# Ten feed-forward steps of a Mamba-2 plus gated FFN kernel: seven 128-wide products for eight in the first matrix product

## The chip, the core and the metric

The kernel runs on one core of one Trainium2 chip. The metric is the device time of one execution in microseconds (us); the runs of the kernel before took 368.01, 369.35 and 369.48 us, the median is 369.35.

Engines are named as in the profile: PE (TensorE matmuls), PEld (its weight loads), DVE (VectorE, called V in the code), ACT (ScalarE), POOL (GpSimd, called G), SP (the queue of most DMAs).

## The reference, cut to what matters

```python
# x: (4, 8, 768, 32), a: (4, 8, 768), B and C: (4, 8, 768, 16)
# w_in: (256, 2048), w_out: (2048, 256), all float32
def reference(x, a, B, C, w_in, w_out):
    y = mamba2_ssd(x, a, B, C)              # a scan in chunks; per chunk y_intra + y_inter
    t = y.transpose(0, 2, 1, 3).reshape(4 * 768, 256)
    h = t @ w_in                            # 3072 x 2048
    g = h * cos(h)
    return g @ w_out                        # 3072 x 256
```

The change concerns `h = t @ w_in` for part of the tokens.

## The kernel before

The 768 positions are cut into six chunks (NC = 6) of 128, for all four batches together: 512 tokens a chunk. The feed-forward part of a chunk takes 16 steps (NF = 16), so there are 96 steps, n = 0 to 95. From chunk 1 on, a step (u, j) takes one half u of the chunk's tokens (4 batches x 64 positions = 256 tokens) and 256 of the 2048 inner columns (pair j of eight). In it:

- `first(n)` (L659) computes hp(n), 256 inner columns x 256 tokens over 256 model columns, as a 128 x 512 tile of one PSUM bank: four matmuls of 128 x 256. The profile counts each float32 matmul as two records, so eight. The banks of hp have the tag "h", of which there are two, so hp(n) needs the bank that hp(n-2) leaves.
- `wind(n)`: ACT makes the whole number of turns k from hp (L666), DVE the remainder w (L672).
- `gate(n)`: ACT takes the sine, which is cos(h) (L681).
- `gated(n)`: DVE multiplies, gT = hp * cos (L686). This is the last reader of hp(n). Then POOL makes four sums and differences of the four 128 x 128 quarters of gT(n) in three instructions (`differ`: L711, L713, L714).
- `seven(n)` (L767) multiplies gT by w_out. It does a product of 2 x 2 blocks in seven block products instead of eight (the Winograd form of Strassen's scheme): 7 matmuls of 128 x 128, 14 records. It runs two steps late (LAG = 2), so PE's order is hp(n), seven(n-2), hp(n+1), seven(n-1), and so on. The seven partial results of eight steps stay in two PSUM banks; after the eighth (j = 7) ACT copies them to SBUF (L776, L777) and, in a later step, DVE adds them up in four instructions (L784) and SP sends them out (L787). These four additions are held in the list `unsummed`; steps with f = 10 and 11 leave it alone.

The order on every engine is the order in which the Python loop at the end of the kernel emits the calls, since the scheduling is by hand (`manual_schedule`). For step n of the last chunk the loop emits: first(n), wind(n), gate(n), gated(n), then `unsummed`, then seven(n-2). So DVE's queue is w(n), gT(n), [L784 x4], w(n+1), gT(n+1), and ACT's is k(n), sine(n), [L776, L777], k(n+1), sine(n+1). The scan of a chunk (lines L375 to L629: decays, reach, turned, state, g, y) is worked off in the steps of the chunk before, so the last chunk's 16 steps, n = 80 to 95, have only feed-forward work. Steps 88 to 95 ("final") keep their partial results in three banks: `shared` (L798 to L803) adds up what both output halves need before the last step, and `last_step` (L811, L814, L816) does step 95 with eight plain matmuls.

The w_in and w_out tiles lie in SBUF for the whole kernel. The four combinations of w_out that `seven` needs are made by POOL in steps 14 to 22 (`differ_w`, L705).

Of the kernel before, what the change touches and what calls it, by code (L numbers as in the profile page):

```python
# [8 lines left out]
FP32 = mybir.dt.float32  # L9
# [16 lines left out]
def kernel(  # L26
# [42 lines left out]
    def bank(shape, name, tag):  # L69
        return psum.tile(shape, FP32, tag=tag, bufs=2, name=name)  # L70

    def pair(name):

        return psum.tile([P, 2, 4 * P], FP32, tag="scan", bufs=2, name=name)
# [570 lines left out]
    def turn_of(n):  # L645

        c, f = divmod(n, NF)
        return (f % 2, f // 2) if c == 0 else divmod(f, NJ)
# [30 lines left out]
    def gate(n):  # L679
        cos = turns[n]  # L680
        ACT.activation(cos, cos, AF.Sin, bias=quarter, scale=TWO_PI)  # L681
# [25 lines left out]
    def differ(n):  # L707
# [5 lines left out]
        G.tensor_tensor(out=d[:, 2], in0=g[:, 0], in1=d[:, 0], op=ALU.subtract)  # L713
        G.tensor_tensor(out=d[:, 3], in0=g[:, 2], in1=d[:, 2], op=ALU.subtract)  # L714

    unit_rows = out.rearrange("(s q k i) m -> q k i s m", s=2, q=2, i=W)

    def second(n):
# [20 lines left out]
    def seven(n):  # L739

        c = n // NF
        u, j = turn_of(n)
        final = n >= NC * NF - NJ
        if j == 0:


            if final:
                lo, hi = (pair("o")[:, 0].rearrange("p (q m) -> p q m", m=P) for _ in range(2))
                mid = bank([P, 4, P], "o", "o")
                o[c, u] = (mid, lo, hi, {1: mid[:, 0], 6: mid[:, 1], 7: mid[:, 2], 5: mid[:, 3],  # L750
                                         2: lo[:, 0], 3: lo[:, 1], 4: hi[:, 0]})
            else:
                lo, hi = (bank([P, 4, P], "o", "o") for _ in range(2))
                o[c, u] = (lo, hi, {1: lo[:, 0], 6: lo[:, 1], 2: lo[:, 2], 7: hi[:, 0],
                                    5: hi[:, 1], 4: hi[:, 2], 3: hi[:, 3]})
        at = o[c, u][-1]
        g = gT.pop(n)
        if n == NC * NF - 1:
            last_step(g, *o[c, u][1:3])
            return  # L760
        d = gd.pop(n)
        w = {1: w4[:, j, 0, 0], 2: w4[:, j, 1, 0], 3: w4[:, j, 1, 1], 4: wd[3][:, j],
             5: wd[0][:, j], 6: wd[2][:, j], 7: wd[1][:, j]}
        a_ = {1: g[:, 0], 2: g[:, 2], 3: d[:, 3], 4: g[:, 3], 5: d[:, 0], 6: d[:, 2], 7: d[:, 1]}
        starts = (1, 2, 4) if final else (1, 7)
        for q in (1, 2, 6, 7, 5, 4, 3):
            PE.matmul(at[q], lhsT=a_[q], rhs=w[q], start=(j == 0 and q in starts),  # L767
                      stop=(j == NJ - 1), skip_group_check=True)
        if final and j == NJ - 2:
            shared(o[c, u][0])  # L770
        if j < NJ - 1:
            return

        sum_ = two.tile([P, 7, P], FP32, tag="sum", bufs=1, name="sum")
        ps = two.tile([P, 7, P], FP32, tag="ps", bufs=1, name="ps")
        ACT.copy(out=ps[:, 0:3], in_=o[c, u][0][:, 0:3])  # L776
        ACT.copy(out=ps[:, 3:7], in_=o[c, u][1])  # L777

        def rest():
            for dst, a_, b_ in ((sum_[:, 0:2], ps[:, 1:3], ps[:, 0:1]),  # L780
                                (sum_[:, 5:7], ps[:, 3:5], sum_[:, 0:1]),
                                (sum_[:, 3:5], ps[:, 5:3:-1], sum_[:, 5:6]),
                                (sum_[:, 2:3], ps[:, 6:7], sum_[:, 6:7])):
                V.tensor_tensor(out=dst, in0=a_, in1=b_.to_broadcast([P, dst.shape[1], P]),  # L784
                                op=ALU.add)
            for s in range(2):
                nc.sync.dma_start(out=unit_rows[s, 2 * c + u], in_=sum_[s * W:(s + 1) * W, 1:5].rearrange(  # L787
                                      "p (t h) m -> p t (h m)", t=2))

        unsummed.append(rest)  # L790
# [151 lines left out]

    AHEAD = 4

    def first_steps():

        grade("in", 1)
        for q in range(2):
            weights(1, q)
        states_of = []  # L950
        first(0, lambda: states_of.extend(finish0(1)))
        take_s1, add_s1 = states_of
        join("in", 1)
        rests = [grade("out", 0, later=True)]
        wind_k(0)
        take_s1()
        rests.pop()()
        wind_w(0)
        first(1)
        join("out", 0)  # L960
        wind_k(1)
        gate(0)
        wind_w(1)
        gate(1)
        gated(0)
        gated(1)
        first(2, tag=None)
        rests = [grade("in", 2, later=True)]
        wind_k(2)
        rests.pop()()  # L970
        clip_cut()
        wind_w(2)
        rests = [grade("out", 1, later=True)]
        join("in", 2)
        first(3, tag=None)
        gate(2)
        wind_k(3)
        rests.pop()()
        rests = [grade("in", 3, later=True)]
        gated(2)  # L980
        join("out", 1)
        second(0)
        wind_w(3)
        gate(3)
        rests.pop()()
        rests = [grade("out", 2, later=True)]
        join("in", 3)
        gated(3)
        second(1)
        clip_all()  # L990
        return add_s1, rests
# [7 lines left out]
    for n in range(AHEAD, NC * NF + LAG):  # L999
        c, f = divmod(n, NF)  # L1000
        if n < NC * NF:

            if c > 0 and f in (loads_of := (6, 7, 8, 9) if c == 1 else (0, 1, 2, 3)):
                load(c + 2, loads_of.index(f))
            if n in (NF - 4, NF - 3):
                load_arow(n - NF + 8)
            if n == NF - 2:
                for k in (4, 5):
                    for s in range(2):
                        load_x(k, s)  # L1010
            if n in (NF - 1, NF):
                load_along(2, (2 * (n == NF), 2 * (n == NF) + 1))
            for e, i in chunks_at(n, "along"):
                load_along(e + 1, (2 * i, 2 * i + 1))
            first(n)
            closing = f == NF - 1 and 1 <= c < NC - 1
            take_y = finish2(c + 1) if closing else None
            wind(n)
            if closing:
                take_y(0)  # L1020
            for e, s in chunks_at(n - 1, "turn"):
                turn2(e, s)
            for k in units_at(n, 2):
                turn_unit(k)
            if n + 1 in piece:
                rests_of.append(grade(*piece[n + 1], later=True))
            gate(n)
            while len(rests_of) > (n == AHEAD):
                rest = rests_of.pop(0)
                if rest:  # L1030
                    rest()
            joins = n in piece and piece[n] in held
            if joins:
                join(*piece[n])

            behind = [lambda at=at: decays2(*at) for at in decays_at(n)]
            behind += [lambda k=2 * c - 1 + i: add_state(k) for c, i in chunks_at(n, "state")]
            behind += [lambda c=c, b=2 * s + p: reaches(c, b) for c, s in chunks_at(n, "reach")
                       for p in range(2)]
            behind += [lambda at=at: turn_blocks(*at) for at in chunks_at(n, "turn")]  # L1040
            behind += [lambda k=k, p=p: decays0(k, p) for k, at in unit_at.items()
                       for p in range(2) if at[0][p] == n]
            behind = [lambda k=2 * c + i, q=q: weights(k, q) for c, i in chunks_at(n, "weigh")
                      for q in range(2)] + behind
            behind = [lambda k=k: weights(k, 1) for k in units_at(n - 1, 3)] + behind
            if not joins and behind:
                behind.pop(0)()
            gated(n)
            if closing:
                take_y(1)  # L1050
            if n == NF + 7:
                weigh0(5)
            if add_s and (n == NF - 5 or units_at(n - 1, 4)):
                exchange = add_s()
                add_s = None
            if n == NF + 9:
                exchange()
            for do in behind:
                do()
            if f not in ((10, 11, 12) if c == 1 else (10, 11)):  # L1060
                for do in unsummed:
                    do()
                unsummed.clear()
            for k, ((_, last_), *_) in unit_at.items():
                if last_ == n:
                    weigh0(k)
        for i, js in differ_at.get(n, ()):
            differ_w(i, js)
        if n == AHEAD + 1:
            second(AHEAD - LAG)  # L1070
        if n >= LAG and n != AHEAD:
# [53 lines left out]
```

## Time and profile before

| | before |
|---|---|
| device time, median of three runs | 369.35 us (368.01 to 369.48) |
| the profiled execution: device time | 367.37 us |
| its span, first to last instruction | 365.2 us |
| around the span | 2.17 us |
| PE busy | 359.7 us (98%) |
| DVE busy | 249.6 us (68%) |
| POOL busy | 204.5 us (56%) |
| ACT busy | 177.8 us (49%) |
| mean granted TensorE clock | 0.999 |

The page of the profile describes one execution. Busy time counts neither waiting nor DMA issue. In a group of instructions, `out<-in` names the tiles, then come the shape, the count, the busy time, the mean ns of one, and after the bar the idle time of the engine just before these instructions with what ended it. In a timeline each line gives the start (us from the start of the span), the duration, the engine, the line, the operation and the count.

### The profile page before, as it was taken

What the parts mean: (1) busy time and instruction counts of PE and PEld (TensorE: products, weight loads), DVE (VectorE), ACT (ScalarE), POOL (GpSimd) and SP (SyncE); (2) the same over time, 40 slices, a digit from 0 to 9 for tenths busy, and PEclk for the clock granted to TensorE, in tenths of its full rate; (3) what the DMA queues carried; (4) which work ended last, traced back from release to release, by engine and by line L of the source; (5) the groups of instructions that cost most, each with busy time, mean ns of one, the idle gap of its engine ahead of it and who ended that gap; (6) DMA issues with size and microseconds to landing.
All of it is one profiled execution on the core that took longest, in us unless ns stands there. A gap on an engine that the chain in (4) does not pass through costs nothing.

```text
span 365.2 us, 9749 instructions
## 1 busy us (share of the span) xinstructions
PE 359.7 (98%) x3902; PEld 324.8 (89%) x3902; DVE 249.6 (68%) x420; ACT 177.8 (49%) x324; POOL 204.5 (56%) x331
## 2 busy tenths in 40 slices
PE   8999999999999999999999999999999999999995
PEld 5788888888999999999989999989999999999995
DVE  7799998488868747967735977754876363644463
ACT  4588766454454355534345444335553534443442
POOL 6567666679766544447734456744355443554441
PEclk9999999999999999999999999999999999999999
DMA  8997865692664455316034210010000010010011
GB/s 146 294 334 154 203 139 72 105 129 64 133 98 65 92 106 72 69 39 121 9 56 62 47 50 22 2 44 5 22 11 0 2 31 2 2 29 3 0 29 31
DMA packets 97324, 26.39 MB, mean 72 GB/s; under 512 B 87328, under 2 KB 93184, under 8 KB 97280
## 3 DMA queue, kind: packets, MB, share of 16 engines
q1 hardware_dynamic: 96032, 25.38, 34.6%
q8 instruction: 31, 0.51, 0.6%
q10 hardware_dynamic: 1248, 0.39, 0.5%
q14 instruction: 13, 0.11, 0.1%
HBM read 22.36 MB, written 3.34 MB: 70 GB/s over the span
## 4 chain that ended last, share of the span: by engine, by line
PE 89%; DVE 4%; POOL 3%; ACT 2%; issue 2%; ACTq 0%; POOLq 0%; DVEq 0%
PE hp L659 42%; PE o L767 33%; PE o L729 5%; PE y L629 2%; PE g L603 1%; PE y L477 1%; DVE mag L261 1%; PE y L617 1%; DVE mag L263 1%; POOL gd L711 1%; PE g L456 1%; PE a_ps L364 1%; PE warm L84 1%; DVE w L672 1%; POOL gd L713 1%
## 5 line engine op out<-in xcount | busy, mean ns | idle before, releaser
L659 PE MATMUL hp<-yT,w_in 128*128 128x256 f32 x768 | 182.7, 381 | 0.3 <-DVE gT L686 0.3
L659 PEld LDWEIGHTS hp<-yT,w_in 128*128 128x128 f32 x768 | 139.5, 190 | 18.2 <-issue 1.0
L711 POOL TENSOR_TENSOR gd<-gT 128x256 f32<-128x256 f32 x79 | 59.8, 757 | 111.9 <-DVE gT L686 102.5
L672 DVE SCALAR_TENSOR_TENSOR w<-hp,k 128x512 f32<-128x512 f32 x96 | 66.1, 688 | 71.4 <-ACT k L666 71.3
L681 ACT ACTIVATE w<-w,quarter 128x512 f32<-128x512 f32 x96 | 69.4, 723 | 71.8 <-DVE w L672 71.5
L666 ACT ACTIVATE k<-hp 128x512 int32<-128x512 f32 x96 | 57.2, 596 | 94.3 <-PE hp L659 94.1
L686 DVE TENSOR_TENSOR gT<-hp,w 128x512 f32<-128x512 f32 x96 | 65.6, 683 | 35.1 <-ACT w L681 33.2
L767 PE MATMUL o<-words,gd 128*128 128x128 f32 x474 | 65.9, 275 | 0.1
L767 PEld LDWEIGHTS o<-words,gd 128*128 128x128 f32 x474 | 59.3, 192 | 0.3 <-POOL gd L713 0.3
L767 PEld LDWEIGHTS o<-w_out,gT 128*128 128x128 f32 x316 | 47.2, 191 | 4.1
L767 PE MATMUL o<-w_out,gT 128*128 128x128 f32 x316 | 48.4, 276 | 0.0
L714 POOL TENSOR_TENSOR gd<-gT,gd 128x128 f32<-128x128 f32 x79 | 44.0, 557 | 6.2
L713 POOL TENSOR_TENSOR gd<-gT,gd 128x128 f32<-128x128 f32 x79 | 38.1, 483 | 6.2
L767 PE MATMUL o<-words,gT 128*128 128x128 f32 x158 | 30.6, 275 | 0.0
L767 PE MATMUL o<-w_out,gd 128*128 128x128 f32 x158 | 30.6, 275 | 0.0
L729 PE MATMUL o<-w_out,gT 128*128 128x256 f32 x128 | 29.9, 379 | 0.0
L375 DVE TENSOR_TENSOR_SCAN lam<-arow,unit 128x512 f32<-128x512 f32 x20 | 28.0, 1400 | 0.0
L729 PEld LDWEIGHTS o<-w_out,gT 128*128 128x128 f32 x128 | 24.2, 190 | 3.3
L767 PEld LDWEIGHTS o<-words,gT 128*128 128x128 f32 x158 | 24.0, 192 | 0.0
L767 PEld LDWEIGHTS o<-w_out,gd 128*128 128x128 f32 x158 | 24.0, 192 | 0.0
L465 DVE TENSOR_TENSOR m<-g,lam 128x512 f32<-128x512 f32 x24 | 16.2, 681 | 0.7 <-PE g L456 0.5
L784 DVE TENSOR_TENSOR sum<-ps,sum 128x256 f32<-128x256 f32 (+1 forms) x27 | 15.1, 586 | 0.6
(109 smaller groups left out, 274.7 us busy)
## 6 DMA issues: line engine op xcount, KB each, us to landing
words<-in_moe_w_in_dram SPq DMA_DIRECT2D x8, 512.0 KB
words<-in_moe_w_out_dram SPq DMA_DIRECT2D x8, 512.0 KB
xr<-in_x_dram SPq DMA_DIRECT2D x24, 128.0 KB
arow<-a_cut SPq DMA_DIRECT2D x10, 256.0 KB
arow<-a_cut SPq DMA_DIRECT2D x10, 252.0 KB
out_dram<-sum SPq DMA_DIRECT2D x18, 128.0 KB
bc<-in_B_dram SPq DMA_DIRECT2D x24, 64.0 KB
blocks<-in_B_dram SPq DMA_DIRECT2D x16, 32.0 KB
```

Of the source, the lines that this page charges most:

```text
L375: V.tensor_tensor_scan(out=lams[k][:, p, hs].rearrange(flat), data0=rows_.rearrange(flat), data1=unit0[:, hs].rearrange(flat), initial=0.0 ...
L465: V.tensor_tensor(out=m, in0=gs[k, q][:, :, 0:2 * P].rearrange("p k (s i) -> p k s i", s=2), in1=l, op=ALU.mult)
L659: PE.matmul(to_[:, e], lhsT=w_in[:, k, fs], rhs=y[:, k], start=(k == 0), stop=(k == KT - 1), skip_group_check=True)
L666: ACT.activation(k, hp[n], AF.Copy, bias=0.25, scale=INV_2PI)
L672: V.scalar_tensor_tensor(out=w, in0=hp[n], scalar=INV_2PI, in1=k, op0=ALU.mult, op1=ALU.subtract)
L681: ACT.activation(cos, cos, AF.Sin, bias=quarter, scale=TWO_PI)
L686: V.tensor_tensor(out=gT[n], in0=hp.pop(n), in1=cos, op=ALU.mult)
L711: G.tensor_tensor(out=d[:, 0:2], in0=g[:, 1:2].to_broadcast([P, 2, P]), in1=g[:, 3::-3], op=ALU.subtract)
L713: G.tensor_tensor(out=d[:, 2], in0=g[:, 0], in1=d[:, 0], op=ALU.subtract)
L714: G.tensor_tensor(out=d[:, 3], in0=g[:, 2], in1=d[:, 2], op=ALU.subtract)
L729: PE.matmul(o[c, u][:, t], lhsT=g[:, 2 * e + t], rhs=w_out[:, 2 * j + e], start=(j == e == t == 0), stop=(j == NJ - 1 and e == 1), skip_gr ...
L767: PE.matmul(at[q], lhsT=a_[q], rhs=w[q], start=(j == 0 and q in starts), stop=(j == NJ - 1), skip_group_check=True)
```

## The change

For steps 83 to 92 (`sevens`), hp(n) is computed by `first7` in seven products of 128 x 128 (14 records) instead of four of 128 x 256 (8 records).

- Four combinations of w_in (`wid`) are made by POOL: 16 instructions of 128 x 256, one in each step of chunk 3 (n = 48 to 63), behind `differ(n)` in the queue.
- Four combinations of yT (`yd`) are made by DVE in steps 80 and 81: four instructions of 128 x 256, two a step, behind gT.
- PE's order in a step is product 6 (to its own bank), 1 (to quarter 0 of the hp bank), 7, 5, 4 (to a third bank), 3 and 2 (to quarters 1 and 0 of the hp bank). ACT copies product 1 to SBUF after the second product. Then DVE makes the four quarters of hp in four instructions (128 x 128, 128 x 256, 128 x 256, 128 x 128); the third and fourth write into the hp bank. The two extra banks are the same for all ten steps, apart from one move of the first of them at step 91.
- In these steps gate and gated are emitted one step later: behind first(n+1), ahead of wind(n+1). So DVE's queue is sums(n), gT(n-1), w(n), sums(n+1), gT(n), w(n+1), and ACT's is copy(n), sine(n-1), k(n), copy(n+1).
- `unsummed` isn't worked off in these steps. What step 89 leaves is added up in step 93; before it was in step 92.
- In the final steps the three banks are laid out otherwise, and the products of `seven` are issued in the order 1, 2, 4, 6, 7, 5, 3 instead of 1, 2, 6, 7, 5, 4, 3.

```diff
+    win4 = w_in.rearrange("p k (j e f) -> p k j e f", j=NJ, e=2)
+    wid, yd = [], {}
+    def differ_in(i, js):
+        if i == len(wid):
+            t = conv.tile([P, 2 * WC, 2], U32, tag="words", bufs=8, name="wid")
...
+        g = [win4[:, k, js, e] for k in range(2) for e in range(2)]
+        a_ = (g[1], g[1], g[0], g[2])[i]
+        b_ = (g[3], g[0], wid[0][:, js], wid[min(i, 2)][:, js])[i]
+        G.tensor_tensor(out=wid[i][:, js], in0=a_, in1=b_, op=ALU.subtract)
+    def differ_y(c, i):
+        if i == 0:
+            yd[c] = ms[2].rearrange("p (i u m) -> p i u m", i=4, u=2)
...
+        V.tensor_tensor(out=d[:, i], in0=a_, in1=b_,
+                        op=ALU.add if i in (1, 2) else ALU.subtract)
+    def first7(n, at6, at):
+        c, f = divmod(n, NF)
+        u, j = turn_of(n)
+        hp[n] = bank([P, TB], "hp", "h")
+        to_ = hp[n].rearrange("p (q m) -> p q m", q=4)
...
+        dst = {6: at6, 1: to_[:, 0], 7: at[:, 0], 5: at[:, 1], 4: at[:, 2], 3: to_[:, 1],
+               2: to_[:, 0]}
+        def product(q):
+            PE.matmul(dst[q], lhsT=w[q], rhs=y_[q], start=(q in (6, 1, 7)), stop=True,
+                      skip_group_check=True)
+        parts = ms[3].rearrange("p (t q m) -> p t q m", t=2, q=4)[:, n % 2]
+        add = dict(op=ALU.add)
+        for q in (6, 1):
+            product(q)
+        ACT.copy(out=parts[:, 0], in_=to_[:, 0])
+        for q in (7, 5, 4, 3, 2):
+            product(q)
+        V.tensor_tensor(out=parts[:, 1], in0=at6, in1=parts[:, 0], **add)
+        V.tensor_tensor(out=parts[:, 2:4], in0=at[:, 0:2],
+                        in1=parts[:, 1:2].to_broadcast([P, 2, P]), **add)
+        V.tensor_tensor(out=to_[:, 2:4], in0=at[:, 2:0:-1],
+                        in1=parts[:, 2:3].to_broadcast([P, 2, P]), **add)
+        V.tensor_tensor(out=to_[:, 1], in0=to_[:, 1], in1=parts[:, 3], **add)
@@ seven
-                lo, hi = (pair("o")[:, 0].rearrange("p (q m) -> p q m", m=P) for _ in range(2))
-                mid = bank([P, 4, P], "o", "o")
+                t = pair("o").rearrange("p b (q m) -> p b q m", m=P)
+                mid, hi = t[:, 0], t[:, 1]
+                lo = bank([P, 4, P], "o", "o")
...
-        for q in (1, 2, 6, 7, 5, 4, 3):
+        for q in (1, 2, 4, 6, 7, 5, 3) if final else (1, 2, 6, 7, 5, 4, 3):
@@ ahead of the loop
+    sevens = range(NC * NF - 13, NC * NF - 3)
+    late, at_ = [], {}
+    def first_of_seven(n):
+        if n == sevens[0]:
+            at_.update(six=pair("m6")[:, 0, 0:P], rest=pair("m")[:, 0, 0:3 * P].rearrange(
+                "p (q m) -> p q m", m=P))
+        if n == NC * NF - NJ + LAG + 1:
+            at_["six"] = bank([P, 4, P], "m6", "o")[:, 0]
+        first7(n, at_["six"], at_["rest"])
+    def finish_late():
+        while late:
+            n = late.pop()
+            gate(n)
+            gated(n)
@@ in the loop
-            first(n)
+            if n in sevens:
+                first_of_seven(n)
+            else:
+                first(n)
+            finish_late()
...
-            gate(n)
+            if n not in sevens:
+                gate(n)
...
-            gated(n)
+            if n in sevens:
+                late.append(n)
+            else:
+                gated(n)
...
-            if f not in ((10, 11, 12) if c == 1 else (10, 11)):
+            for i in range(2):
+                if n in (sevens[0] - 3, sevens[0] - 2):
+                    differ_y(c, 2 * (n - sevens[0] + 3) + i)
+            if n not in sevens and f not in ((10, 11, 12) if c == 1 else (10, 11)):
                 for do in unsummed:
                     do()
...
+        if n // NF == NC - 3:
+            i, q = divmod(f, 4)
+            differ_in(i, slice(2 * q, 2 * q + 2))
```

More of the change, by code (lines that the diff above doesn't have):

```diff
@@ L714, in differ @@
         G.tensor_tensor(out=d[:, 3], in0=g[:, 2], in1=d[:, 2], op=ALU.subtract)
+    win4 = w_in.rearrange("p k (j e f) -> p k j e f", j=NJ, e=2)
[3 more added lines that the diff above has]
+            t = conv.tile([P, 2 * WC, 2], U32, tag="words", bufs=8, name="wid")
+            wid.append(t.rearrange("p a w -> p (a w)").bitcast(FP32)
+                       .rearrange("p (j f) -> p j f", j=NJ))
+        g = [win4[:, k, js, e] for k in range(2) for e in range(2)]
+        a_ = (g[1], g[1], g[0], g[2])[i]
+        b_ = (g[3], g[0], wid[0][:, js], wid[min(i, 2)][:, js])[i]
+        G.tensor_tensor(out=wid[i][:, js], in0=a_, in1=b_, op=ALU.subtract)
@@ new lines, in differ_y @@
+    def differ_y(c, i):
+        if i == 0:
+            yd[c] = ms[2].rearrange("p (i u m) -> p i u m", i=4, u=2)
+        d = yd[c]
+        y11, y12, y21, y22 = (yT[c][:, :, k, h * P:(h + 1) * P] for k in range(2) for h in range(2))
+        a_ = (y12, y22, y22, y21)[i]
+        b_ = (y11, y12, d[:, 0], d[:, 2])[i]
+        V.tensor_tensor(out=d[:, i], in0=a_, in1=b_,
[5 more added lines that the diff above has]
+        to_ = hp[n].rearrange("p (q m) -> p q m", q=4)
+        w = {1: win4[:, 0, j, 0], 2: win4[:, 1, j, 0], 3: wid[3][:, j], 4: win4[:, 1, j, 1],
+             5: wid[0][:, j], 6: wid[2][:, j], 7: wid[1][:, j]}
+        d, y = yd[c][:, :, u], yT[c][:, u].rearrange("p k (h i) -> p k h i", h=2)
+        y_ = {1: y[:, 0, 0], 2: y[:, 1, 0], 3: y[:, 1, 1], 4: d[:, 3], 5: d[:, 0], 6: d[:, 2],
+              7: d[:, 1]}
+        dst = {6: at6, 1: to_[:, 0], 7: at[:, 0], 5: at[:, 1], 4: at[:, 2], 3: to_[:, 1],
[16 more added lines that the diff above has]
+        V.tensor_tensor(out=to_[:, 1], in0=to_[:, 1], in1=parts[:, 3], **add)
```

## The prediction

> **What bounds the kernel now.** I read the page first (busy time by engine), then what TensorE waited for, then the chain that ended last.
>
> ```profile
> PE 359.7 (98%) x3902; PEld 324.8 (89%) x3902; DVE 249.6 (68%) x420; ACT 177.8 (49%) x324; POOL 204.5 (56%) x331
> ```
>
> ```profile
> PE warm L84 <- PEq L1109: 0.8, 1, 0.8
> PE g L456 <- ACT cT L399: 0.5, 1, 0.5
> PE hp L659 <- DVE gT L686: 0.3, 1, 0.3
> ```
>
> ```profile
> 320.25 1.56 PE o L767 x14
> 321.81 1.73 PE hp L659 x8
> ```
>
> PE is busy for the whole span and waited 1.6 us for others in all. The chain is PE alone, in steps of 1.73 + 1.56 = 3.29 us. So time off PE is time off the kernel, as long as nobody makes PE wait. Fourteen 128-wide records take 1.56, eight 256-wide ones 1.73: 0.17 us is the most that one step can gain.
>
> Next the DVE groups with shapes kept apart, and the timeline of the place where the seven-product steps begin (step 83's hp is the eight records from 315.07 on; gT(82) is at 315.95).
>
> ```profile
> L784 DVE TENSOR_TENSOR sum<-ps,sum 128x256 f32<-128x256 f32 x18 | 11.7, 652 | 0.6
> L814 DVE TENSOR_TENSOR ob<-o,ps 128x256 f32<-128x256 f32 x2 | 0.8, 421 | 0.3 <-PE o L811 0.3
> L801 DVE TENSOR_TENSOR ps<-ps 128x256 f32<-128x256 f32 x1 | 0.4, 425 | 0.0
> L800 DVE TENSOR_TENSOR ps<-ps 128x128 f32<-128x128 f32 x1 | 0.3, 293 | 0.4 <-ACT ps L798 0.4
> ```
>
> ```profile
> 315.95 0.69 DVE L686 TENSOR_TENSOR gT<-hp,w 128x512 f32<-128x512 f32 x1 [0.86 <-ACT w L681]
> 316.56 0.41 DVE L784 TENSOR_TENSOR sum<-ps 128x256 f32<-128x256 f32 x1
> 316.78 0.78 POOL L711 TENSOR_TENSOR gd<-gT 128x256 f32<-128x256 f32 x1 [1.49 <-DVE gT L686]
> 316.80 0.61 PE L767 MATMUL o<-w_out,gT 128*128 128x128 f32 x4
> 317.00 1.90 DVE L784 TENSOR_TENSOR sum<-ps,sum 128x256 f32<-128x256 f32 x3
> 317.06 0.60 ACT L666 ACTIVATE k<-hp 128x512 int32<-128x512 f32 x1 [1.21 <-PE hp L659]
> 318.36 1.89 PE L659 MATMUL hp<-yT,w_in 128*128 128x256 f32 x8
> 318.82 0.68 DVE L672 SCALAR_TENSOR_TENSOR w<-hp,k 128x512 f32<-128x512 f32 x1
> ```
>
> DVE is held by L784 until 318.9, so w(83) comes 1.1 us late; before, that cost nothing, since PE needed gT(83) only much later. Delays between engines: last hp record issued 316.80 to k 317.06, 0.26; in the last step (timeline) gT ends 359.41 and its PE load begins 359.46, 0.05; ACT to DVE 0.03; DVE to a DVE instruction that needs it 0.04; unrelated DVE rows overlap by 0.07. A load runs 0.11 ahead of its matmul.
>
> [...] the 384-wide copy L776 took 460 [...], the 256-wide L636 379 [...]. I take 0.27. [...] The trace agrees: L784 652 ns beside POOL, the same shape 425 alone. [...] The built kernel's queues agree: product 3 carries a wait on ACT's copy of another quarter of its bank, and product 7 of step 84 one on DVE, the two products behind it none, so it waits for the third sum of step 83.
>
> **The change part by part** (us).
>
> *Removed:* 10 x (1.73 - 1.56) = -1.7.
>
> *The running state, steps 85 to 92.* Let product 1 start at 0. It ends at 0.22; copy 0.48 to 0.75; sum 1 0.78 to 1.07; sum 2 needs product 4 (0.89 + 0.26) and ends at 1.57. Product 3's load, due at 0.78, waits for the copy until 0.80; product 2 ends at 1.36. Sum 3 waits for it, as it writes to its bank: 1.62 to 2.04. Sum 4 to 2.37, gT(n-1) 2.30 to 2.99. gT(n-1) frees the bank of hp(n+1): load at 3.04, product 1 at 3.15. PE alone would be there at 3.12. k(n) ends at 3.00, w(n) at 3.72, and the next sum 1 is due at 3.93. So DVE just fits: 7 x 0.03 = +0.2. The unshown thing is a DVE write to PSUM (sums 3 and 4). Lower bound 0: PE sets 3.12 anyway; upper bound 0.2 a step (0.1 an instruction, a third more than the row): +1.4. I take the rows' price.
>
> *Hand-over, steps 83 to 85.* Sums(83) stand behind L784 in DVE's queue, and everything of step 84 behind them. Sum 1 318.82 to 319.11, sum 2 to 319.57, sum 3 to 320.03, sum 4 to 320.36, k(83) 320.39 to 320.99, w(83) 321.02 to 321.71, sums(84) 321.64 to 323.18 (four instructions and three gaps), gT(83) 323.11 to 323.80, product 1 of step 85 at 323.80 + 0.16 = 323.96. Without waits it is due at 315.07 + 2 x 3.12 + 0.22 = 321.53. That is 2.4 lost. PE sits it out in four places: product 6 of 84 (for sum 1 of 83), product 7 (for sum 3), product 3 (copy(84), which stands behind k(83) on ACT), product 1 of 85. If one of these waits is finer than I read it, the last one grows, since the DVE chain is the same. The four yd instructions in steps 80 and 81 have two SBUF inputs beside POOL and put back w by 0.1 each (as the first two L784, 0.41 + 0.04 + 0.83 behind gT, against the 1.05 idle ahead of w): +0.2. Together +2.6. Bounds: 1.6 if L784 runs at 425 and 293 without POOL (it would end 0.8 earlier) and yd costs nothing; 3.2 if yd is blocked each time.
>
> *Step 89.* ACT has L776 and L777 behind k(89). k ends at 3.00, L777 can't end before 3.98, and copy(90), due at 3.63, follows it; product 3 of step 90 waits till 4.27 instead of 3.93: +0.3 (0 to 0.5).
>
> *Back to eight, step 93.* The first matmul of L659 writes to the hp bank at once, not as its second product: it needs gT(91) at 3.04 and its load is due at 2.81: +0.2.
>
> *Tail.* L784 now follows gT(93), not gT(92), with w(94) behind it. As in the lines above, w then begins 2.87 after gT(93), gT(94) 1.54 later, and POOL's second piece (L713) ends 2.1 after gT(94) begins (gT(83) 320.36, L713 322.00 + 0.46). Seven(94) runs straight behind seven(93) and needs that piece as its fourth product: by the sum it comes 0.25 late with its load; before, L784 lay a step earlier and seven(94) found it ready. +0.3 (0 to 0.5).
>
> *Chunk 3.* Sixteen POOL instructions of about 0.78 (L711 757, L705 826). POOL has some 1.7 of 3.29 in a step, so they fit; SP and ACT have nothing behind them. [...] In step 49 gT ends at 207.37 and the load of hp(51) begins at 207.51: 0.14 to spare, while `wid` meets L784's end at 204.7 and can push it by 0.3 to 0.5. In the four steps of the scans (L375, 1.22 each, and L714 blocked to 1.4 beside them) POOL would need 1.7 + 0.78 + 1.22 = 3.7 of 3.29; its results have about 2 us to spare. I take +0.4 (0 to 1.3).
>
> *SP.* The output of L784 goes out one step later (step 93), still three steps before the end: 0.
>
> Sum: -1.7 + 0.2 + 2.6 + 0.3 + 0.2 + 0.3 + 0.4 = +2.3. The profiled execution would go from a span of 365.2 to 367.5, and with 2.17 around it from 367.37 to 369.7. The median shown is 369.35, 2.0 above that execution; I add the difference to the median: 371.6.
>
> **The rivals.**
>
> *Not slower: [...]* Of my costs, 0.8 (L784 at the hand-over), 0.2 (yd), 0.3 (tail) and 0.4 (chunk 3) hang on DVE and POOL meeting. If they pass each other, 1.7 goes: +0.6, 369.9, no measurable change. For it: L784's fastest rows are 415 and 278. Against it: POOL follows every gT by 0.14, just when L784 runs. It decides once less than 1.25 of the 1.7 appears. Chance 0.32.
>
> *VectorE becomes the bound.* If sums 2 to 4 take 0.1 more each, the loop is 3.45 rather than 3.15 and eight steps lose 0.3: +2.4 on top, 374.0. For it: by the rows' price the loop (3.15) is already longer than PE's step (3.12). Against: the PSUM read costs nothing in L814. Chance 0.14.
>
> *POOL falls behind in chunk 3* by more than its 2 us: +1.7 on top, 373.3. Chance 0.06.
>
> *The change does only what it says*, all else hidden: -1.7, 367.6. Against it stands the DVE queue at 318.9. Chance 0.04.
>
> **How the numbers follow.** Forecast 371.6 with 0.44 (its own range 370.7 to 372.6). About 0.5%, 1.85 us, is what a measurement of this kernel tells from no change, so slower means above 371.2: forecast 0.36, VectorE 0.14, POOL 0.06, and 0.04 [...], 0.60. Same: 0.28 + 0.08 + 0.01 = 0.37. Faster: 0.03. The range 369.2 to 373.9 leaves out the last rival, the lower end of the first and the upper half of VectorE's.
>
> **What would show it.** After: a hp step of 14 records at 1.56; PE waits on DVE in steps 84 and 85 of some 2.4 in sum; w to w on DVE of about 3.15 in steps 86 to 92; L784 before the first sum. Wrong if PE waits under 1 us there, if the sums' rows are over 0.5 for 256, or if chunk 3 grows by over 1 us.

## The result and the profile after

| | before | after |
|---|---|---|
| device time, median | 368.74 us (367.70 to 369.88) | 371.3 us (370.62 to 371.72) |
| profiled execution: device time | 367.37 us | 370.71 us |
| its span | 365.2 us | 368.9 us |

The ratio is 1.0062, with a 95% interval of 1.0042 to 1.0083: the change costs 2.56 us by the medians and 2.3 us by the ratio (1.5 to 3.1). The forecast was 371.6, slower by 2.3. The two profiled executions lie 3.7 us apart by their spans. Each is one execution: that of before lies 1.4 below its median, that of after 0.6, and the time outside the span is 2.2 us before and 1.8 after. So what follows adds up to 3.7, and some tenths more or less in a sum of a whole execution mean nothing.

The first lines of the page after:

```profile
span 368.9 us, 9960 instructions
...
PE 359.7 (98%) x3962; PEld 325.2 (88%) x3962; DVE 267.0 (72%) x464; ACT 179.3 (49%) x334; POOL 216.6 (59%) x347
```

PE has 60 records more (ten steps of 14 for 8) and is busy for the same 359.7 us. The 1.7 us that the products save don't show in this figure: while nobody waits, the records overlap (two of 128 x 128 last 0.39 us, and the next start 0.22 after them), and where PE waits this overlap goes (two that have waited last 0.46 to 0.49, below), so the same work counts as more busy time. The waits tell more. What TensorE waited for after the change, longest in sum first:

```profile
PE m L758 <- DVE m L768: 0.8, 1, 0.8
PE warm L84 <- PEq L1203: 0.8, 1, 0.8
PE hp L659 <- DVE gT L686: 0.8, 2, 0.4
...
PE m L758 <- DVE hp L771: 0.4, 1, 0.4
PE hp L758 <- DVE gT L686: 0.4, 1, 0.4
PE hp L758 <- ACT m L765: 0.3, 1, 0.3
```

L758 is a product of `first7`. Its four waits are the four places which the prediction named for steps 84 and 85: product 6 (for the first sum, L768), product 7 (for the third, L771), product 1 of step 85 (for gT) and product 3 (for ACT's copy, L765). In this list they are 1.9 us. By the starts of the steps (below) 2.86 are lost: the list counts a wait from the modelled end of the matmuls before, 0.17 after the next are due, and the two records that have waited take 0.1 longer (0.49 for 0.39), so some 0.27 comes on top of each of the four. The timeline of after shows them in order; start and duration come first:

```profile
316.68 0.69 DVE L686 TENSOR_TENSOR gT<-hp,w 128x512 f32<-128x512 f32 x1 [0.86 <-ACT w L681]
317.29 0.42 DVE L844 TENSOR_TENSOR sum<-ps 128x256 f32<-128x256 f32 x1
317.74 1.89 DVE L844 TENSOR_TENSOR sum<-ps,sum 128x256 f32<-128x256 f32 x3
319.55 0.28 DVE L768 TENSOR_TENSOR m<-m,m 128x128 f32<-128x128 f32 x1
319.88 0.49 PE L758 MATMUL m<-m,wid 128*128 128x128 f32 x2 [0.83 <-DVE m L768]
320.95 0.71 PE L758 MATMUL m<-m,wid 128*128 128x128 f32 x4 [0.35 <-DVE hp L771]
321.34 0.60 ACT L666 ACTIVATE k<-hp 128x512 int32<-128x512 f32 x1 [4.62 <-DVE hp L773]
321.84 0.26 ACT L765 COPY m<-hp 128x128 f32<-128x128 f32 x1
322.15 0.49 PE L758 MATMUL hp<-yT,wid 128*128 128x128 f32 x2 [0.27 <-ACT m L765]
324.17 0.68 DVE L686 TENSOR_TENSOR gT<-hp,w 128x512 f32<-128x512 f32 x1
325.00 0.46 PE L758 MATMUL hp<-yT,w_in 128*128 128x128 f32 x2 [0.35 <-DVE gT L686]
```

gT(82) is followed by the four additions of a finished unit (L844, L784 before), and only then, at 319.55, by the first sum of step 83. ACT has nothing to do for 4.62 us until the fourth sum gives it hp(83). gT(83) comes at 324.17, and product 1 of step 85 starts at 325.00. Product 1 of step 83 started at 315.90. Two steps of PE alone are 2 x 3.12 = 6.24, so 9.10 - 6.24 = 2.86 us are lost here.

Behind the hand-over the steps should have taken PE's 3.12. They take 3.27 to 3.28 (the step from 90 to 91 takes 3.37). One turn of this running state, in the timeline of after:

```profile
328.28 0.46 PE L758 MATMUL hp<-yT,w_in 128*128 128x128 f32 x2
...
328.83 0.27 ACT L765 COPY m<-hp 128x128 f32<-128x128 f32 x1 [0.60 <-PE hp L758]
...
329.13 0.29 DVE L768 TENSOR_TENSOR m<-m,m 128x128 f32<-128x128 f32 x1 [0.17 <-ACT m L765]
...
329.52 0.42 DVE L769 TENSOR_TENSOR m<-m 128x256 f32<-128x256 f32 x1
...
330.05 0.43 DVE L771 TENSOR_TENSOR hp<-m 128x256 f32<-128x256 f32 x1
...
330.52 0.30 DVE L773 TENSOR_TENSOR hp<-hp,m 128x128 f32<-128x128 f32 x1
...
330.73 0.68 DVE L686 TENSOR_TENSOR gT<-hp,w 128x512 f32<-128x512 f32 x1
...
331.55 0.46 PE L758 MATMUL hp<-yT,w_in 128*128 128x128 f32 x2
```

The list of waits shows next to nothing of it: PE loses 0.15 in each step and nearly all of that passes as a matmul that began and ended later (0.46 for 0.39). It is read from the starts of product 1 alone: 325.00, 328.28, 331.55, 334.83, 338.10, 341.38, 344.75, 348.04.

### The profile page after: what moved, and what is told of

It is laid out like the page before. It is cut to its first block, busy times and chain, and to the rows that moved or that the text cites. A ratio compares the mean times of both kernels' runs of the same rounds, so it can differ in the third digit from the quotient of the medians.

```text
span 368.9 us, 9960 instructions
## 1 busy us (share of the span) xinstructions
PE 359.7 (98%) x3962; PEld 325.2 (88%) x3962; DVE 267.0 (72%) x464; ACT 179.3 (49%) x334; POOL 216.6 (59%) x347
## 4 chain that ended last, share of the span: by engine, by line
PE 77%; DVE 8%; SPq 5%; issue 3%; ACT 3%; POOL 2%; DMA 2%; DVEq 0%; ACTq 0%; POOLq 0%
PE hp L659 33%; PE o L827 29%; PE o L788 3%; PE m L758 2%; PE hp L758 2%; PE y L629 2%; DMA bc<-in_C_dram 1%; DVE w L672 1%; PE g L603 1%; DVE sum L844 1%; SPq L147 1%; DVE mag L261 1%; SPq L165 1%; DVE gT L686 1%; ACT k L666 1%
## 5 line engine op out<-in xcount | busy, mean ns | idle before, releaser
L659 PE MATMUL hp<-yT,w_in 128*128 128x256 f32 x688 | 163.9, 382 | 0.9 <-DVE gT L686 0.8
L659 PEld LDWEIGHTS hp<-yT,w_in 128*128 128x128 f32 x688 | 125.0, 190 | 17.5 <-issue 1.0
L827 PE MATMUL o<-words,gd 128*128 128x128 f32 x474 | 66.1, 275 | 0.1
L827 PEld LDWEIGHTS o<-words,gd 128*128 128x128 f32 x474 | 59.3, 192 | 0.4 <-POOL gd L713 0.3
L827 PEld LDWEIGHTS o<-w_out,gT 128*128 128x128 f32 x316 | 46.4, 191 | 3.6
L827 PE MATMUL o<-w_out,gT 128*128 128x128 f32 x316 | 48.4, 276 | 0.0
L714 POOL TENSOR_TENSOR gd<-gT,gd 128x128 f32<-128x128 f32 x79 | 40.5, 512 | 6.2
L713 POOL TENSOR_TENSOR gd<-gT,gd 128x128 f32<-128x128 f32 x79 | 40.4, 512 | 6.2
L827 PE MATMUL o<-words,gT 128*128 128x128 f32 x158 | 30.5, 275 | 0.0
L827 PE MATMUL o<-w_out,gd 128*128 128x128 f32 x158 | 30.5, 275 | 0.0
L788 PEld LDWEIGHTS o<-w_out,gT 128*128 128x128 f32 x128 | 24.2, 190 | 3.3
L827 PEld LDWEIGHTS o<-w_out,gd 128*128 128x128 f32 x158 | 24.0, 192 | 0.0
L827 PEld LDWEIGHTS o<-words,gT 128*128 128x128 f32 x158 | 24.0, 192 | 0.0
L844 DVE TENSOR_TENSOR sum<-ps,sum 128x256 f32<-128x256 f32 (+1 forms) x27 | 15.5, 600 | 0.6
```

The lines of the kernel that those rows point to most:

```text
L659: PE.matmul(to_[:, e], lhsT=w_in[:, k, fs], rhs=y[:, k], start=(k == 0), stop=(k == KT - 1), skip_group_check=True)
L788: PE.matmul(o[c, u][:, t], lhsT=g[:, 2 * e + t], rhs=w_out[:, 2 * j + e], start=(j == e == t == 0), stop=(j == NJ - 1 and e == 1), skip_gr ...
```

## The experiments

Every kernel below computes all of the output. In the one called "the parts alone" the combinations are made and not used. Each ratio is to the kernel before on the same chip (its median is 367.84 for the start at step 85, the parts alone, `wid` in other steps and the third bank in a pair's half, and 368.17 for the others). A step "starts" with its product 1.

### Where the loss at the hand-over comes from

**Sevens from step 85 on.** The additions then lie two steps ahead of the first sums. `yd` is still made in steps 80 and 81.

```diff
-    sevens = range(NC * NF - 13, NC * NF - 3)
+    sevens = range(NC * NF - 11, NC * NF - 3)
```

> The seven-product steps begin at step 85 instead of 83 (eight of them, 85 to 92); all else as in the changed kernel. Theory: the 2.9 us that TensorE loses at the hand-over are due to the four additions of L844 in step 82, which stand in VectorE's queue ahead of the first sums. Begun at 85, the first sums wait only for gT(84), some 0.5 us. So 2.4 us come back, two steps lose their saving of 0.17 each, and one interval of the slow running state (0.15) goes: 2.2 us less than the changed kernel, some 369.1 us. Rival: the loss lies in the change of order itself (gT behind the next sums), wherever it is made: then it stays near 2.9 us and the time is 371.5 us.

369.05 us, ratio 1.0033 (1.0021 to 1.0045). Steps 85 to 87 start at 322.36, 325.56 and 329.53: 7.17 - 6.24 = 0.93 lost for 2.86. The rest of the steps take the same 3.27 to 3.28. The remainder is not zero: DVE still has gT(84) (323.12 to 323.81) ahead of the first sum, which starts 1.37 after product 1 instead of 0.85, and the third sum of step 85 waits 0.46 more behind the second (until 325.00), for which the trace names nothing but the second sum itself.

**The additions on GpSimd.** All ten steps stay; the four additions go to POOL, one in each of the steps 82 to 85.

```diff
-                V.tensor_tensor(out=dst, in0=a_, in1=b_.to_broadcast([P, dst.shape[1], P]),
-                                op=ALU.add)
+                eng.tensor_tensor(out=dst, in0=a_, in1=b_.to_broadcast([P, dst.shape[1], P]),
+                                  op=ALU.add)
...
+                yield
...
+            if n in range(NC * NF - 14, NC * NF - 10):
+                if n == NC * NF - 14:
+                    by_pool = unsummed.pop()(True)
+                next(by_pool)
```

> The changed kernel (start at 83), with the four additions that VectorE makes in step 82 made by GpSimd instead, one in each of steps 82 to 85. Nothing else is moved. Theory (these additions, ahead of the first sums in VectorE's queue, make the hand-over cost 2.9 us): the hand-over falls to 0.5 to 0.9 us, so 2.0 to 2.4 us less than the changed kernel, 0.2 to 0.6 us over the kernel before. Rival (the hand-over costs what it does by the new order itself): no gain, 2.6 us over the kernel before.

368.98 us, ratio 1.0024 (1.0014 to 1.0034). The timeline of this kernel (product 1 of step 83 at 316.35):

```profile
317.12 0.69 DVE L686 TENSOR_TENSOR gT<-hp,w 128x512 f32<-128x512 f32 x1 [0.86 <-ACT w L681]
...
317.73 0.28 DVE L768 TENSOR_TENSOR m<-m,m 128x128 f32<-128x128 f32 x1
...
323.18 0.46 PE L758 MATMUL hp<-yT,w_in 128*128 128x128 f32 x2 [0.34 <-DVE gT L686]
```

The first sum follows gT at once, product 1 of step 85 comes at 323.18, and 6.83 - 6.24 = 0.59 is lost. So the place of the additions in DVE's queue is worth 2.86 - 0.59 = 2.27, and the 0.59 is what the one gT ahead of the first sums costs with two hp banks; with a third bank the same two steps take 6.34 (315.58 to 321.92 in the last kernel below). The medians give less, 0.8 slower than before where after was 2.56, so 1.75 of the 2.27 (by the ratios 0.9 where after was 2.3, so 1.4), within their intervals. The additions don't keep POOL long: 0.72 to 0.73 each at 128 x 256.

### Chunk 3

**The parts alone.** `wid` and `yd` are made in the same steps as in after, no step uses them.

```diff
-    sevens = range(NC * NF - 13, NC * NF - 3)
+    sevens = range(0)
```

> The combinations of w_in (GpSimd, chunk 3) and of yT (VectorE, steps 80 and 81) are made as in the changed kernel, but all hp are computed in eight products as before, so they are not used; the banks and product order of the final steps are as changed. Theory: the GpSimd work in chunk 3 costs TensorE 0.65 us once, at step 51, where gT(49) is late for the hp bank; the yT work and the tail cost nothing: 0.65 us over the kernel before, 369.4 us. Rival: the shift seen in the profile at step 51 is made up for later, or isn't due to the added GpSimd work: 368.7 us, as before.

368.74 us, ratio 1.0030 (1.0015 to 1.0044). By the ratio that is 1.1 us (0.6 to 1.6). In the trace 0.65 is lost at step 53 beyond what the start-up explains, and up to step 95 nothing more. (The prediction and the expectations count this step as 51 and its gT(51) as 49: in the traces the hp that waits is number 53.) In after the loss is 0.65 as well, at the same place; the first line is of before:

```profile
203.83 1.36 DVE L784 TENSOR_TENSOR sum<-ps,sum 128x256 f32<-128x256 f32 x3
```

```profile
203.03 0.88 DVE L844 TENSOR_TENSOR sum<-ps 128x256 f32<-128x256 f32 x1
...
203.94 1.89 DVE L844 TENSOR_TENSOR sum<-ps,sum 128x256 f32<-128x256 f32 x3
...
204.78 0.90 POOL L730 TENSOR_TENSOR wid<-w_in 128x256 f32<-128x256 f32 x1
...
208.15 1.10 PE L659 MATMUL hp<-yT,w_in 128*128 128x256 f32 x4 [0.41 <-DVE gT L686]
```

Before, the three additions took 1.36 here; now, with `wid` beside them on POOL, they take 1.89. gT(51) comes 0.63 later, and the first matmul of step 53 waits for it.

**The same in other steps.** `wid` in steps 40 to 47 and 56 to 63.

```diff
-        if n // NF == NC - 3:
-            i, q = divmod(f, 4)
+        wid_at = [*range(40, 48), *range(56, 64)]
+        if n in wid_at:
+            i, q = divmod(wid_at.index(n), 4)
```

> The changed kernel with the sixteen GpSimd instructions that make the combinations of w_in in steps 40 to 47 and 56 to 63 instead of 48 to 63, so none of them stands near step 51. Theory: the 0.65 us at step 51 go and nothing takes their place, since the scan steps 55 to 58 lost nothing in the changed kernel: 370.65 us. Rival: GpSimd's added work costs wherever it is put[...]: 371.3 us or more.

370.45 us, ratio 1.0078 (1.0065 to 1.0091). In the trace the additions take 1.36 again and step 53 waits for nothing, so the 0.65 is gone there. The time doesn't show it: by the ratio this kernel is 2.9 us (2.4 to 3.3) slower than before, and after was 2.3 (1.5 to 3.1). What happens at step 53 is shown by the trace; that the time gains by it is not shown.

### What holds the running state at 3.27

The theory: each step needs, one after the other, copy, four sums, gT(n-1), and gT(n-1) frees the bank of hp(n+1). A third hp bank cuts that loop. The rival: DVE has too much work.

**A third bank, in a pair's unused half.**

```diff
-        hp[n] = bank([P, TB], "hp", "h")
+        hp[n] = (at_["third"] if (n - sevens[0]) % 3 == 2 else bank([P, TB], "hp", "h"))
...
+            both_ = pair("m")
+            at_.update(six=pair("m6")[:, 0, 0:P], third=both_[:, 1],
+                       rest=both_[:, 0, 0:3 * P].rearrange("p (q m) -> p q m", m=P))
```

> The changed kernel with three PSUM banks in turn for hp of the ten steps instead of two (the third is the unused half of a pair that the change holds anyway). Theory: in the running state product 1 waits for gT of the step before, the last reader of the bank; with three banks it needs gT of two steps before, the steps fall from 3.275 to TensorE's own 3.12 us (7 x 0.15 = 1.1 us) and the wait at step 93 (0.45 us) goes: 1.5 us less than the changed kernel, some 369.8 us. Rival: VectorE is simply full with 3.27 us of work and waits in each step; a bank more changes nothing, 371.3 us.

375.56 us, ratio 1.0213 (1.0200 to 1.0226): a miss. What TensorE waited for in this kernel:

```profile
PE m L758 <- DVE w L672: 2.2, 3, 0.7
PE m L758 <- ACT m L765: 1.2, 3, 0.4
```

Product 7 writes to one half of the pair, w and the copy read the other half, and the waits go by the pair. So the edit brought 3.4 us of waits of its own. One interval without such a wait was 3.13. For 3.4 us the granted clock fell to 0.50 as well (last section), but that doesn't make the miss: one of the four executions had a mean clock of 1.000 and took 375.63 us.

**A third bank in a pair by itself.** Products 6, 7, 5 and 4 then share one bank, and the move at step 91 is that of the third bank.

```diff
+        hp[n] = (at_["third"] if n % 3 == 2 else bank([P, TB], "hp", "h"))
...
+            at_["third"] = pair("hp")[:, 0]
+            four = pair("m")[:, 0].rearrange("p (q m) -> p q m", m=P)
+            at_.update(six=four[:, 3], rest=four[:, 0:3])
...
-            at_["six"] = bank([P, 4, P], "m6", "o")[:, 0]
+            at_["third"] = bank([P, TB], "hp", "o")
```

> The third bank again, but kept apart: in the third-bank run the third bank was one half of a pair whose other half takes products 7, 5 and 4, and product 7 waited for the readers of the pair's other half. Here products 6, 7, 5 and 4 share one bank, and the third bank for hp is alone in its pair. Theory (the bank of hp sets the running state of the changed kernel): steps of 3.12 to 3.15 us instead of 3.275, 1.0 us less; step 93 without its wait, 0.45 less; the hand-over without its last wait, 0.3 to 0.6 less. So some 1.9 us less than the changed kernel and 0.7 us over the kernel before. Rival (VectorE is full at 3.27 us a step): steps stay at 3.27 us, and only the 0.45 goes: 2.1 us over the kernel before.

374.43 us, ratio 1.0153 (1.0129 to 1.0177). Steps 85 to 90 come 3.13 to 3.16 apart, so the loop is cut, and DVE does the same work in that time: the theory holds, the rival falls. But the time is worse, a miss by some 5 us, with two new waits and, after the first of them, 3.4 us at a granted clock of 0.50 (last section). What TensorE waited for in this kernel:

```profile
PE m L758 <- DVE hp L771: 1.8, 1, 1.8
PE o L827 <- DVE gT L686: 1.6, 1, 1.6
```

The first: product 6 of step 84 now waits for the third sum of step 83, as it shares the bank that this sum reads. The second: the final steps (88 to 95) take over the pair, and its last reader is gT(89), in the third bank by n % 3 == 2; step 90 waits for it.

**The third bank without this second wait** (used in steps 85, 88 and 91), and otherwise as in the kernel just above.

```diff
+        hp[n] = (at_["third"] if n % 3 == 1 else bank([P, TB], "hp", "h"))
```

> The changed kernel with the third bank alone as edit, used in steps 85, 88 and 91. The hand-over is as in the earlier run with a third bank kept apart: product 6 of step 84 shares its bank with 7, 5 and 4 and so waits for the third sum of step 83, 1.8 us, after which TensorE's clock was granted at 0.50 for some 3.4 us. Theory: the steps run at 3.13 us, step 93 doesn't wait; against the changed kernel 1.0 + 0.45 us less, but 1.5 us more for the halved clock: about as the changed kernel, 2.6 us over the kernel before. Rival: the halved clock had another cause than the wait of 1.8 us and doesn't come again: 0.9 us over the kernel before.

369.85 us, ratio 1.0050 (1.0031 to 1.0068): 1.9 us over the kernel before, between the 2.6 of the theory and the 0.9 of the rival. The clock stayed at 1.00 in this trace. The wait of 1.8 at step 84 is there again, that at step 90 is not. The waits of this kernel:

```profile
PE m L758 <- DVE hp L771: 1.8, 1, 1.8
```

Steps 85 to 90 come 3.13 to 3.19 apart.

### Put together

**Sevens from 85, `wid` moved, third bank by n % 3 == 2**, and then **all ten steps with the additions on POOL instead of the later start**. The edits are those above; the first also keeps `yd` in steps 80 and 81, and has:

```diff
+    sevens = range(NC * NF - 11, NC * NF - 3)
+        wid_at = [*range(40, 48), *range(56, 64)]
+        hp[n] = (at_["third"] if n % 3 == 2 else bank([P, TB], "hp", "h"))
```

> Start at step 85, the w_in combinations away from step 51, and the third bank kept apart, together: eight seven-product steps with no cost that is known to be left but a short hand-over. Theory: 8 x 0.17 = 1.4 us saved, 0.1 to 0.5 us of hand-over: 0.9 to 1.3 us less than the kernel before (a ratio near 0.997). Rival: the costs aren't separate, and TensorE waits elsewhere for what is taken away: as the kernel before or slower.

> All ten steps from 83 on, with the additions of step 82 on GpSimd, the w_in combinations away from step 51 and the third bank kept apart. Theory: 10 x 0.17 = 1.7 us saved, 0.2 to 0.6 us of hand-over left: 1.1 to 1.5 us less than the kernel before (ratio near 0.9965). Rival: VectorE, with 3.0 us of work in each step of 3.12, can't make up what the hand-over puts it back by, and TensorE waits in each step: no gain.

370.12 us, ratio 1.0054 (1.0035 to 1.0074), and 369.66 us, ratio 1.0050 (1.0032 to 1.0068): both miss, and in both traces TensorE waits 1.6 us for gT(89) in step 90.

**The same two with the third bank in steps 85, 88 and 91.**

```diff
+        hp[n] = (at_["third"] if n % 3 == 1 else bank([P, TB], "hp", "h"))
```

> As the run of three edits together (start at 85), with the third bank used in steps 85, 88 and 91. Theory: 8 x 0.17 = 1.4 us saved, 0.1 to 0.5 us of hand-over: 0.9 to 1.3 us less than the kernel before. Rival: as the kernel before.

> As the run with everything but the start, except that the third bank serves steps 85, 88 and 91 instead of 83, 86, 89 and 92, so that its last reader before the final steps (gT(88)) is done a step earlier than step 90, where those steps take its pair. Theory: the 1.6 us that TensorE waited there for gT(89), and the 1.7 us by which that run's profile is longer than its sum, go: 1.1 to 1.5 us less than the kernel before (ratio near 0.9965). Rival: another wait of the same size takes its place at step 90, from ACT's copies of the partial results: no gain over the kernel before.

The first takes 367.79 us, ratio 0.9995 (0.9985 to 1.0004), as before: a miss. The second takes 367.06 us, ratio 0.9973 (0.9957 to 0.9988): 1.0 us less than the kernel before (0.4 to 1.6), and the fastest of all. That bears out the theory; of the rival, a wait of 1.6 us at step 90 from ACT's copies, 0.6 came. What TensorE waited for in it, all of L659, L758 and L827:

```profile
PE hp L659 <- DVE gT L686: 0.4, 1, 0.4
PE hp L758 <- ACT m L765: 0.3, 1, 0.3
...
PE o L827 <- POOL gd L713: 0.2, 1, 0.2
```

Its timeline at two successive product 6 and at the sums between them:

```profile
321.70 0.39 PE L758 MATMUL m<-m,wid 128*128 128x128 f32 x2
...
323.09 0.29 DVE L768 TENSOR_TENSOR m<-m 128x128 f32<-128x128 f32 x1
...
324.62 0.68 DVE L686 TENSOR_TENSOR gT<-hp,w 128x512 f32<-128x512 f32 x1
...
324.85 0.39 PE L758 MATMUL m<-m,wid 128*128 128x128 f32 x2
325.08 0.39 PE L758 MATMUL hp<-yT,w_in 128*128 128x128 f32 x2
```

Product 1 (325.08) starts while gT is still at work (until 325.30): with two banks it would have to wait for it. From step 84 on the steps come 3.13 to 3.16 apart. One doesn't: step 90 to 91 takes 3.74, where copy(90) stands behind the unit's two copies on ACT, and product 3 waits for it (0.3, the second line above). Of the 1.7 saved, 0.6 goes there, and counted from step 83 step 93 comes 0.83 earlier than before. In the trace not all of this reaches the end: PE takes 0.26 longer from step 93 on, where seven(94) waits for POOL (the third line above), and the end comes 0.3 later behind the last addition, so that from step 83 to the end it is 49.88 us for 50.15, and the two spans are both 365.2. The 1.0 rests on the times of the executions, 8 against 30; one trace of each shows 0.27.

## Why the prediction was right, and where its sum was off

The direction and the mechanism held: what was saved on PE went at the hand-over, as DVE's queue has the additions ahead of the sums. That 371.6 lies only 0.3 from the median is in part luck. The sum was 1.4 below that of the traces, and the profiled execution of before, which it starts from, was taken as 2.0 below the median (1.4 with all seven executions). Term by term, forecast against the trace of after:

| term | forecast | measured |
|---|---|---|
| saved on PE | -1.7 | -1.7 (14 records in the time foreseen: 3.13 a step where nothing waits) |
| hand-over, with yd | +2.6 | +2.86 |
| running state and step 89, steps 85 to 92 | +0.2 and +0.3 | +1.2 (23.04 less 7 x 3.12 = 21.84) |
| step 93 | +0.2 | +0.45 |
| tail on PE | +0.3 | 0.0 |
| chunk 3 | +0.4 | +0.65 |
| end of the span, behind PE | none | +0.3 (from the last addition to the end, 3.58 for 3.30) |
| sum | +2.3 | +3.7 to 3.8, against 3.7 in the spans and 2.56 in the medians |

- **Hand-over.** Of the 0.26 too little, the two sets of sums are 0.26 (1.68 for 1.54, and 1.59 for 1.47 up to gT), DVE to ACT 0.08 (0.11 for 0.03), and `yd` gives 0.07 back (it pushed gT(82) by 0.13, not 0.2). That the additions' place in the queue is the cause is shown by the kernels that move them to POOL or start two steps later.
- **The running state is the term that was mis-sized: +0.2, "7 x 0.03", where about 1.1 came.** The loop was the right one and bounds the step, but it is 3.275, not 3.15 (from w to w on DVE 3.27, where the prediction named 3.15 as its sign). In the turn shown above copy starts 0.55 after product 1 (0.48 in the prediction; its 0.27 for the copy was an estimate, and the ten rows have 0.266 in the mean), sum 1 0.85 (0.78), sum 3 1.77 (1.62), sum 4 2.24 (2.08), gT 2.45 (2.30), and the next product 1 3.27. So 0.07 is late with the copy and 0.08 in the sums. The 0.07 comes with the wait itself: a product 1 that has waited takes 0.46 for 0.39, and where it hasn't, in the last kernel above, the copy starts 0.48 behind it (321.92 to 322.40). The 0.08 lies for the most part in the gaps ahead of sums 2 and 3 (last section). The stated upper bound of 1.4 held it; the value taken was too near the lower end. What it means: a step of seven products in this order takes 3.275 against 3.29 of eight, and the change saves 0.015 in each, not 0.17.
- **Step 89.** Step 90 to 91 takes 3.37 for 3.275: 0.1, not 0.3, since ACT had slack left by the slower loop. With the third bank it was 0.6 (3.74), twice the price.
- **VectorE as the bound** was a rival with a price of 3.45 a step. The third bank shows that DVE has time for 3.13; it was the chain, not the load.
- **DVE and POOL pass each other** was the likeliest rival. It fell: the four additions at the hand-over took as long as before (0.42 and 1.89 us), two of the four `yd` took 0.83 and 0.95 for 0.42, and the additions in chunk 3 1.89 for 1.36.
- **Chunk 3.** At the place foreseen (step 53, which the prediction calls 51), by the additions beside POOL; that they would end 0.3 to 0.5 later was an estimate, and it was 0.53 (1.89 for 1.36). The four scan steps lost nothing.
- **Step 93** (0.45 for 0.2) is the late gT(91) of the slower loop.
- **Tail.** POOL's piece was late as foreseen: it ends at 361.92, and the product of seven(94) that needs it, whose load was due at 361.81, starts its load at 361.98. The 0.0 is luck. Before, the last step waited about as long for gT(95) (until 359.41), and now it doesn't.
- **End of the span.** The prediction had no term for it. The first of the last two additions now comes 0.34 ahead of the second, and 0.73 before, so their outputs follow closer. The traces with about 0.34 all have 3.6 us to the end, those with 0.6 and 0.7 have 3.3; that the one causes the other is not tested.

The medians' 2.56 is 1.1 less than the 3.7 of the spans. The distances of the two executions from their medians (0.8) and the time outside the span (0.4) cover it; it is no term of the table.

## What to carry to other kernels

Before PE work is traded for sums on another engine, follow one turn of the loop that gives a buffer back, through every engine and gap: it must be shorter than the new PE step, by more than the hundredths that a reading leaves out, or the saving doesn't appear. Look at what stands ahead of the first new instruction in the queue it joins, and move that elsewhere; the same change gained 1.0 us once the additions were on POOL, `wid` was made in other steps, a third bank cut the loop, and the bank was given back before the next owner needed it. A buffer added for this purpose has owners before and after it: give it a tile of its own, and check who takes it over and when.

## What the runs showed of the hardware

In the trace of after, two of the four sums on VectorE, L769 and L771, have a second entry of 21 ns ahead of them; both wait for PE beside the sum before. L773, which waits for the sum before alone, has none. The instructions of line L769:

```profile
L769 DVEq EVENT_SEMAPHORE  x10: 21/21/21, 319.9 to 349.2; - x10
L769 DVE TENSOR_TENSOR m<-m x10: 425/425/427, 319.9 to 349.3; 128x256 f32<-128x256 f32 x10
```

Ahead of L769 and L771 the gap to the sum before is 0.10 to 0.11 us, ahead of L773 0.04. (The prediction had 0.08 and 0.05 ahead of the two, the first for product 4.) In two kernels with products 6, 7, 5 and 4 in one bank (the third bank by itself, and the fastest) L769 has no such entry and its gap is 0.03 to 0.04; L771 still has it, with 21 ns and a gap of 0.10 to 0.11. The sums that write to PSUM (L771 and L773) also took a little longer than those that write to SBUF (L769 and L768), 433 ns for 425 and 299 for 289. The groups of after with shapes apart:

```profile
L771 DVE TENSOR_TENSOR hp<-m 128x256 f32<-128x256 f32 x10 | 4.3, 433 | 1.0
L769 DVE TENSOR_TENSOR m<-m 128x256 f32<-128x256 f32 x10 | 4.3, 425 | 1.0
L773 DVE TENSOR_TENSOR hp<-hp,m 128x128 f32<-128x128 f32 x10 | 3.0, 299 | 0.3
L768 DVE TENSOR_TENSOR m<-m,m 128x128 f32<-128x128 f32 x10 | 2.9, 289 | 1.4 <-ACT m L765 1.2
```

That is 8 ns at 256 wide and 10 at 128; the prediction's upper bound for this, an estimate, was 100.

In the traces of two kernels PE also ran for 3.4 us at a granted clock of 0.50. In the kernel with the third bank by itself, busy time by engine in three stretches; the number ahead of the last two is the granted clock:

```profile
320.00:322.00 2.00, 0.61 (x5) 0.62 (x6) 1.49 (x5) 0.22 (x1) 0.00 (x0) 1.00 0.24 55
322.90:326.30 3.40, 3.40 (x18) 3.40 (x17) 2.84 (x7) 1.32 (x2) 0.86 (x2) 0.50 0.01 2
326.30:330.00 3.70, 3.70 (x35) 3.70 (x34) 2.04 (x5) 1.46 (x3) 0.78 (x2) 1.00 0.00 0
```

PE waited 1.8 us up to 321.4, and 1.5 us later it ran 3.4 us at half clock, with 18 records in 3.40 us where the next 3.70 us have 35. The mean clock of this execution, 0.991, is that of two such stretches (below), and its second long wait is that of 1.6 us at step 90. In the kernel with a third bank in a pair's unused half there is a stretch from about 322.4 to 325.8: 0.50 from 323 to 325, 0.68 in the microsecond before and 0.61 in the one behind.

The wait alone doesn't decide. The kernel with the third bank at 85, 88 and 91 had the same 1.8 us wait, and the first two put together the same 1.6 at step 90, and all three kept 1.00 in their traces where these waits are. From 310 to 322 us the trace of after is as busy as that of the pair's half (PE 10.70 and 10.71 of the 12.0), and it kept 1.00 from 314 to 326. The mean clocks of the single executions say the same. A stretch of 3.4 us at 0.50 makes the mean 0.995 (1 - 0.5 x 3.4 / 368), two make it 0.991, as in these traces. Of the six executions with the third bank at 85, 88 and 91 one has 0.995, and took 371.37 us where the others took 369.74 to 369.89. Two of six and three of eight of the first two put together have it, all five of the third bank by itself have 0.995 or 0.991, one each of after (0.995, of 7), the parts alone (0.994, of 17) and `wid` in other steps (0.995, of 5), and none of the 8 of the fastest kernel or of the 76 of before in the experiments. So it comes in some executions of a kernel and not in others. It is most frequent in the third bank by itself (five of five, with waits of 1.8 and 1.6 us) and in the pair's half (three of four, with no wait over 0.8). What decides is not shown.
